# An earlier fetch of one scalar, and a weight decoding whose two engines run one step apart

## The chip, the cores and the metric

The kernel runs on one core of a Trainium2 chip. Its engines work side by side, each through its own list of instructions in order, and wait for each other by semaphores: TensorE (PE in the profile; PEld is its weight load) does the matrix products, VectorE (DVE) and ScalarE (ACT) the elementwise work, GpSimd (POOL) a little setup, and SyncE (SP) issues most transfers. The metric is the device time of one execution in microseconds (us). Three runs of the kernel before took 658.86, 659.36 and 659.38 us, so the median is 659.36.

## The reference

Attention with a soft cap over 2 batches, 12 heads, 448 positions and head size 64; its output, as 896 tokens of 768 features, goes through two gated layers of width 1536:

```
scores = cap * tanh((q @ k.T / sqrt(64)) / cap)
attn   = exp(scores - max);  attn = attn / (sum(attn) + 1e-9)
x      = attn @ v                                  # 896 x 768
x      = (silu(x @ g1) * (x @ v1)) @ o1            # layer 0
out    = (sigmoid(x @ g2) * (x @ v2)) @ o2         # layer 1
```

`cap` is one number. The six weight matrices arrive as 64-bit floats.

## The kernel before

**Precision.** Every operand of a large product is split in a high and a low part (names end in h and l), and three products are summed: high by high, low by high, high by low.

**Weights.** A block of a weight matrix (768 words of 64 bits in each of the 128 partitions, the tile `r`) is turned into its two 32-bit parts by `decode`, which VectorE and ScalarE share: VectorE shifts the top word (`t`, L74), ScalarE rounds it (`c`, L75), VectorE collects the remaining bits (`g`, L77 and L78) and puts the sign back (`c`, L80), ScalarE writes the high part (`wh`, L81), VectorE takes off the exponent and writes the low part (`wl`, L83 and L84). `decode` is a generator. Each of its `yield`s, and one more in `Stream.steps`, ends a step, so a block has four steps. `ws.step()` emits one step; `ws.through(key)` emits all steps up to the end of that block. When a block is done, the load of the block after the next one is issued on SyncE's queue. `("g", 0, 1)` is the gate block of layer 0, columns 128 to 255; `("v", 0, 1)` is the value block of the same columns.

**Attention.** The 24 heads are worked on in 12 pairs (`for i in range(NPAIR)`). For each pair TensorE transposes K and Q (`transposed`), VectorE and ScalarE split them (`qk_parts`: `kh`, `qh`, `kl`, `ql`), TensorE makes the scores of four key chunks (`scores`), ScalarE puts tanh on them with the scale `inv_sb`, which is made from the cap on VectorE (L467 to L471), and then the exponential in two parts (`exponentials`); VectorE adds up exponentials (`sums`), TensorE multiplies with V (`values`: `pv`, and the denominators `pd`), ScalarE and VectorE take the results out of PSUM (`taken_off`: `xu`, `dn`). The denominators travel through memory: `g` is fetched from `dn`, inverted, written to `d` and read back spread over the partitions as `rb` (`inverted`); `normalized` multiplies and splits the result into `xh` and `xl`. The loop is pipelined: in the turn of pair i the sums and values are those of pair i-1, the inversion that of i-2, the normalization that of i-3, the transposes those of i+2. The order of the calls in the loop is the order of the instructions on each engine.

From pair 3 on (`FIRST`), some steps of the weight decoding are emitted in each turn, `NS` = 16 in all: four blocks.

**The passage to the layers.** After the loop the first products of layer 0 are interleaved with the last pair: the gate block over the first batch's tokens, the last pair's values, the value block over the first batch, then both over the second batch (first without the last two pairs), the second gate block over the first batch, and only then the part that needs the last two pairs. `inverted_here(last)` inverts the last denominators on VectorE directly.

**The layers.** TensorE runs without a pause, and the other engines decode blocks ahead of it with `ws.through`.

Of the kernel before, what the change touches and what calls it, by code (L numbers as in the profile page):

```python
# [9 lines left out]
F32 = mybir.dt.float32  # L10
# [9 lines left out]
def attention_then_two_gated_layers(  # L20
# [14 lines left out]
    nc = tc.nc  # L35
# [3 lines left out]
    P = 128  # L39
# [9 lines left out]
    const = ctx.enter_context(tc.tile_pool(name="const", bufs=1))  # L49
# [16 lines left out]
    def decode(r, hi, lo):  # L66

        n = r.shape[1] * r.shape[2]
        w2 = r.rearrange("p k f -> p (k f)").bitcast(U32).rearrange("p (n two) -> p n two", two=2)
        low, top = w2[:, :, 0], w2[:, :, 1]  # L70
        t = wp.tile([P, n], U32, tag="t", name="t", bufs=1)
        c = wp.tile([P, n], U32, tag="c", name="c", bufs=2)
        g = wp.tile([P, n], F32, tag="g", name="g", bufs=1)
        nc.vector.tensor_scalar(t, top, 0x7FFFFFFF, 9, ALU.bitwise_and, ALU.logical_shift_right)  # L74
        nc.scalar.activation(c, t, AF.Relu, bias=bias_sb, scale=4096.0)  # L75
        yield
        nc.vector.tensor_scalar(g.bitcast(U32), top, 0x1FF, None, ALU.bitwise_and)  # L77
        nc.vector.scalar_tensor_tensor(g, low, 2.0**-32, g.bitcast(U32), ALU.mult, ALU.add)  # L78
        yield
        nc.vector.scalar_tensor_tensor(c, top, 0x80000000, c, ALU.bitwise_and, ALU.bitwise_or)  # L80
        nc.scalar.copy(hi, c.bitcast(F32).rearrange("p (k f) -> p k f", k=r.shape[1]))  # L81
        yield
        nc.vector.tensor_scalar(t, c, 0xFF800000, None, ALU.bitwise_and)  # L83
        nc.vector.scalar_tensor_tensor(  # L84
            lo,
            g.rearrange("p (k f) -> p k f", k=r.shape[1]),
            2.0**-20,
            t.bitcast(F32).rearrange("p (k f) -> p k f", k=r.shape[1]),
            ALU.mult,
            ALU.mult,  # L90
        )

    class Stream:
# [11 lines left out]
        def load(self, upto):  # L105
            while self.loaded < min(upto, len(self.keys)):
                key = self.keys[self.loaded]
                src = self.jobs[key][0]
                r = wp.tile([P, src.shape[0] // P, src.shape[1]], I64, tag="r", name="r", bufs=2)
                nc.sync.dma_start(r, src.rearrange("(k p) f -> p k f", p=P))  # L110
                self.raw[key] = r
                self.loaded += 1
# [37 lines left out]
    def products(o, w, bh, bl, u, ks, nk, off=0):  # L150

        for kk in ks:
            for m, (a, x) in enumerate(((w[0], bh), (w[0], bl), (w[1], bh))):
                nc.tensor.matmul(  # L154
                    o,
                    lhsT=a[:, kk - off, :],
                    rhs=x[:, kk, halves[u]],
                    start=(kk == 0 and m == 0),
                    stop=(kk == nk - 1 and m == 2),
                )  # L160
# [8 lines left out]
    def weights():  # L169
        pools, z_tiles = {}, {}  # L170

        def z_part(eb, c):
            def get():
                if eb not in z_tiles:
                    if eb == 0:
                        z_tiles[eb] = [pools["hp"].tile([P, KF, ZB[0]], F32R, name=n) for n in ("zh0", "zl0")]
                    else:
                        z_tiles[eb] = [const.tile([P, KF, ZB[1]], F32R, tag=n, name="z" + n) for n in ("xh", "xl")]
                return [z[:, :, c * ZW : (c + 1) * ZW] for z in z_tiles[eb]]

            return get

        jobs = {}

        def z_job(eb, c):
            e0 = sum(ZB[:eb]) + c * ZW
            jobs["z", eb, c] = (o2[:, e0 : e0 + ZW], z_part(eb, c))

        for layer, (wg, wv) in enumerate(((g1, v1), (g2, v2))):
            for f in range(KF):  # L190
                for kind, w in (("g", wg), ("v", wv)):
                    jobs[kind, layer, f] = (w[:, f * P : (f + 1) * P], None)
                if (layer, f) in early:
                    z_job(0, early.index((layer, f)))
            if layer == 0:
                for e in range(KD):
                    for part in range(2):
                        if part == 0 and (2, e) in early:
                            z_job(0, early.index((2, e)))
                        jobs["o", e, part] = (o1[part * KD * P : (part + 1) * KD * P, e * P : (e + 1) * P], None)  # L200
        for c in range(ZB[1] // ZW):
            z_job(1, c)
        return Stream(jobs), pools, z_tiles
# [93 lines left out]
    ws, pools, z_tiles = weights()  # L297
    with ExitStack() as actx:
        ap = actx.enter_context(tc.tile_pool(name="ap", bufs=2))
        dr = actx.enter_context(tc.tile_pool(name="dr", bufs=2, space=bass.MemoryType.DRAM))  # L300
        fix = actx.enter_context(tc.tile_pool(name="fix", bufs=1))

        warm = ap.tile([P, 512], mybir.dt.bfloat16, tag="x", name="warm", bufs=2)
        nc.vector.memset(warm, 0.0)
# [36 lines left out]
        def load_v(i):  # L341
            b, p = pairs[i]
            tv = vt[i % NV]
            nc.sync.dma_start(tv[:, :, :NB], v[b, 2 * p : 2 * p + 2, :S0].rearrange("h (p r) d -> p h r d", r=NB))
            for j in range(2):
                nc.sync.dma_start(tv[rows[j], j, NB, :], v[b, 2 * p + j, S0:])
# [48 lines left out]
        def sums(i, part):  # L395

            e = ex[i]
            if part == 0:
                es[i] = ap.tile([P, 2, S], F32, tag="es", name="es", bufs=2)
                nc.vector.tensor_tensor(es[i], e[:, 0:2], e[:, 2:4], ALU.add)  # L400
            else:
                nc.vector.tensor_tensor(es[i], es[i], e[:, 4:6], ALU.add)
# [32 lines left out]
        def inverted(i):  # L435
            g = dens.pop(i)
            nc.vector.reciprocal(g, g)
            d = dr.tile([2 * S], F32, tag="d", name="d")
            nc.sync.dma_start(d.rearrange("(p c) -> p c", p=CP), g)
            rb[i] = ap.tile([P, S], F32, tag="rb", name="rb", bufs=2)  # L440
            for j in range(2):
                nc.sync.dma_start(rb[i][rows[j]], d[j * S : (j + 1) * S].unsqueeze(0).to_broadcast([D, S]))

        def inverted_here(i):

            xu[i], d = nd.pop(i)
            rb[i] = ap.tile([P, S], F32, tag="rb", name="rb", bufs=2)
            nc.vector.reciprocal(rb[i], d)

        def normalized(i):  # L450
            b, p = pairs[i]
            x = ap.tile([P, S], F32, tag="x", name="x", bufs=2)
            nc.vector.tensor_tensor(x, xu.pop(i), rb.pop(i), ALU.mult)
            o = slice(b * S, (b + 1) * S)
            nc.vector.tensor_copy(xh[:, p, o], x)
            nc.vector.tensor_tensor(xl[:, p, o], x, xh[:, p, o].bitcast(F32), ALU.subtract)

        cap_sb = const.tile([P, 1], F32, name="cap_sb")
        nc.gpsimd.dma_start(cap_sb, cap.to_broadcast([P, 1]))
        wide_sb = const.tile([1, 1], mybir.dt.int32, name="wide_sb")  # L460
        inv_sb = fix.tile([P, 1], F32, name="inv_sb")
        near_sb = const.tile([P, 1], F32, name="near_sb")
# [9 lines left out]
        qk_parts(0)  # L472
        load(2)
        load_v(1)
        NS, FIRST = 16, 3
        for i in range(NPAIR):
            if i + 3 < NPAIR:
                load(i + 3)
            if i + 2 < NPAIR:
                load_v(i + 2)  # L480
            if i == 1:
                ws.load(2)
            if i > 0:
                sums(i - 1, 1)
            if i > 1:
                inverted(i - 2)
            if i > 2:
                normalized(i - 3)
            scores(i, 0)
            if i == 0:  # L490
                transposed(1)
                qk_parts(1, nc.vector.tensor_copy)
            scores(i, 1)
            exponentials(i, 0)
            if i > 0:
                values(i - 1)
            if i >= FIRST:
                n = NPAIR - FIRST
                for _ in range(NS * (i - FIRST) // n, NS * (i - FIRST + 1) // n):
                    ws.step()  # L500
            sums(i, 0)
            if i > 0:
                taken_off(i - 1)
            scores(i, 2)
            scores(i, NB)
            exponentials(i, 1)
            if i + 2 < NPAIR:
                transposed(i + 2)
                qk_parts(i + 2, nc.vector.tensor_copy)
# [7 lines left out]
        products(begun[0][0][0], w0[0], xh, xl, 0, range(KD), KD)  # L517
        values(last)
        products(begun[0][1][0], w0[1], xh, xl, 0, range(KD), KD)
        inverted_here(last)  # L520
        normalized(last)
        normalized(last - 1)
# [112 lines left out]
```

## Time and profile before

| | before |
|---|---|
| median of 3 runs | 659.36 us |
| the profiled execution's own time | 659.29 us |
| span of its profile (first to last instruction) | 657.5 us |
| PE busy | 642.7 us (98%) |
| DVE busy | 459.1 us (70%) |
| ACT busy | 276.0 us (42%) |
| mean granted TensorE clock | 0.99 of full |

Times of the trace count from the span's start. The rows below are of four kinds. A timeline row gives the start, the duration, the engine, the line, what is written from what, and in brackets the idle time of the engine just before and what ended it; "xN" is N instructions merged. A waits row gives total us, times and the longest. A windows row gives, for a stretch, its length, each engine's busy time, the granted clock (1.00 is 2.4 GHz, 0.50 is 1.2 GHz) and the DMA engines' share. A group row gives the count, the summed busy time and the mean of one in ns. Most of the span is the layers, where TensorE is busy throughout; the attention takes about the first 116 us.

### The profile page before, as it was taken

What the parts mean: (1) busy time and instruction counts of PE and PEld (TensorE: products, weight loads), DVE (VectorE), ACT (ScalarE), POOL (GpSimd) and SP (SyncE); (2) the same over time, 40 slices, a digit from 0 to 9 for tenths busy, and PEclk for the clock granted to TensorE, in tenths of its full rate; (3) what the DMA queues carried; (4) which work ended last, traced back from release to release, by engine and by line L of the source; (5) the groups of instructions that cost most, each with busy time, mean ns of one, the idle gap of its engine ahead of it and who ended that gap; (6) DMA issues with size and microseconds to landing.
All of it is one profiled execution on the core that took longest, in us unless ns stands there. A gap on an engine that the chain in (4) does not pass through costs nothing. (4 is left out here: it accounts for less than half of the span.)

```text
span 657.5 us, 8373 instructions
## 1 busy us (share of the span) xinstructions
PE 642.7 (98%) x3311; PEld 548.3 (83%) x3311; DVE 459.1 (70%) x678; ACT 276.0 (42%) x352; POOL 3.9 (1%) x25
## 2 busy tenths in 40 slices
PE   7999899999999999999999999999999999999996
PEld 4455454799999999999999999999999999999995
DVE  3689899648798777886969767777887773693000
ACT  2988699224344333443434324333443332342000
POOL 2000000000000000000000000000000000000000
PEclk7999899999999999999999999999999999999999
DMA  5644442204433234433344233334342332270111
GB/s 138 196 112 129 110 127 78 65 20 135 134 113 128 96 107 133 134 130 122 112 129 144 97 118 119 100 110 130 99 141 97 97 124 68 67 224 21 43 28 34
DMA packets 99861, 70.86 MB, mean 108 GB/s; under 512 B 29030, under 2 KB 99814, under 8 KB 99814
## 3 DMA queue, kind: packets, MB, share of 16 engines
q1 hardware_dynamic: 98662, 69.80, 34.8%
q8 instruction: 28, 0.46, 0.3%
q10 hardware_dynamic: 1120, 0.45, 0.3%
q14 instruction: 19, 0.16, 0.1%
q0 software_dynamic: 32, 0.00, 0.0%
HBM read 67.40 MB, written 2.79 MB: 107 GB/s over the span
## 5 line engine op out<-in xcount | busy, mean ns | idle before, releaser
L75 ACT ACTIVATE c<-t,bias_sb 128x768 uint32<-128x768 uint32 x72 | 67.7, 940 | 87.1 <-DVE t L74 87.1
L81 ACT CAST wh<-c 128x768 fp32r<-128x768 f32 x60 | 50.3, 839 | 81.2 <-DVE c L80 81.1
L78 DVE SCALAR_TENSOR_TENSOR g<-r,g 128x768 f32<-128x768 uint32 x72 | 69.0, 959 | 2.5
L80 DVE SCALAR_TENSOR_TENSOR c<-r,c 128x768 uint32<-128x768 uint32 x72 | 68.5, 951 | 0.8 <-ACT c L75 0.7
L227 DVE TENSOR_TENSOR sg<-pv,sg 128x448 f32<-128x448 f32 x48 | 29.8, 620 | 49.5 <-PE pv L154 41.6
L84 DVE SCALAR_TENSOR_TENSOR wl<-g,t 128x768 fp32r<-128x768 f32 x60 | 57.5, 959 | 2.1
L228 ACT CAST hh<-sg 128x448 fp32r<-128x448 f32 x48 | 27.2, 567 | 74.2 <-DVE sg L227 74.2
L154 PE MATMUL pg<-xh,wh 128*128 128x448 f32 x144 | 52.8, 367 | 0.3 <-ACT e L385 0.3
L154 PE MATMUL pg<-hl,wh 128*128 128x448 f32 x144 | 53.0, 368 | 0.0
L154 PE MATMUL pg<-hh,wl 128*128 128x448 f32 x144 | 53.0, 368 | 0.0
L154 PE MATMUL pg<-hh,wh 128*128 128x448 f32 x144 | 53.0, 368 | 0.0
L154 PE MATMUL pv<-xh,wh 128*128 128x448 f32 x144 | 52.8, 367 | 0.0
L154 PE MATMUL pv<-yh,wl 128*128 128x448 f32 x144 | 52.7, 366 | 0.0
L154 PE MATMUL pg<-xl,wh 128*128 128x448 f32 x144 | 52.7, 366 | 0.0
L154 PE MATMUL pg<-yh,wh 128*128 128x448 f32 x144 | 52.7, 366 | 0.0
L154 PE MATMUL pg<-yl,wh 128*128 128x448 f32 x144 | 52.7, 366 | 0.0
L154 PE MATMUL pv<-yl,wh 128*128 128x448 f32 x144 | 52.7, 366 | 0.0
L154 PE MATMUL pg<-xh,wl 128*128 128x448 f32 x144 | 52.7, 366 | 0.0
L154 PE MATMUL pg<-yh,wl 128*128 128x448 f32 x144 | 52.7, 366 | 0.0
L154 PE MATMUL pv<-xh,wl 128*128 128x448 f32 x144 | 52.7, 366 | 0.0
L154 PE MATMUL pv<-yh,wh 128*128 128x448 f32 x144 | 52.7, 366 | 0.0
L154 PE MATMUL pv<-xl,wh 128*128 128x448 f32 x144 | 52.7, 366 | 0.0
(98 smaller groups left out, 1274.1 us busy)
## 6 DMA issues: line engine op xcount, KB each, us to landing
r<-in_moe_w_gate_dram SPq DMA_DIRECT2D x24, 768.0 KB, 4.4
r<-in_moe_w_val_dram SPq DMA_DIRECT2D x24, 768.0 KB, 4.2
r<-in_moe_w_out_dram SPq DMA_DIRECT2D x24, 768.0 KB, 4.4
tq<-in_q_dram SPq DMA_DIRECT2D x11, 224.0 KB, 4.0
rb<-d SPq DMA_DIRECT2D x22, 112.0 KB, 2.9
kt<-in_k_dram SPq DMA_DIRECT2D x12, 192.0 KB, 3.2
vt<-in_v_dram SPq DMA_DIRECT2D x12, 192.0 KB, 3.4
out_dram<-ob SPq DMA_DIRECT2D x4, 140.0 KB, 3.7
```

The source lines that it names most:

```text
L75: nc.scalar.activation(c, t, AF.Relu, bias=bias_sb, scale=4096.0)
L78: nc.vector.scalar_tensor_tensor(g, low, 2.0**-32, g.bitcast(U32), ALU.mult, ALU.add)
L80: nc.vector.scalar_tensor_tensor(c, top, 0x80000000, c, ALU.bitwise_and, ALU.bitwise_or)
L81: nc.scalar.copy(hi, c.bitcast(F32).rearrange("p (k f) -> p k f", k=r.shape[1]))
L84: nc.vector.scalar_tensor_tensor(lo, g.rearrange("p (k f) -> p k f", k=r.shape[1]), 2.0**-20, t.bitcast(F32).rearrange("p (k f) -> p k f", ...
L154: nc.tensor.matmul(o, lhsT=a[:, kk - off, :], rhs=x[:, kk, halves[u]], start=(kk == 0 and m == 0), stop=(kk == nk - 1 and m == 2),)
L227: nc.vector.tensor_tensor(sg, vs[u], sg, ALU.mult)
L228: nc.scalar.copy(hh[:, f, halves[u]], sg)
```

## The change

Four edits. The transfer of the cap is the first thing that GpSimd does, ahead of its memory fills. In `decode` the first `yield` stands before ScalarE's rounding instead of behind it, and the third before ScalarE's copy, so that ScalarE's instruction comes in the step after VectorE's that it reads; a block still has four steps. `NS` is 8 instead of 16, so the loop decodes two blocks, and the second gate block is decoded after the loop, ahead of the last inversion, with the second value block behind the last normalizations as the existing call places it. In the loop `normalized(i - 3)` is called ahead of `inverted(i - 2)`.

```
         nc.vector.tensor_scalar(t, top, 0x7FFFFFFF, 9, ALU.bitwise_and, ALU.logical_shift_right)
+        yield
         nc.scalar.activation(c, t, AF.Relu, bias=bias_sb, scale=4096.0)
-        yield
         nc.vector.tensor_scalar(g.bitcast(U32), top, 0x1FF, None, ALU.bitwise_and)
...
         nc.vector.scalar_tensor_tensor(c, top, 0x80000000, c, ALU.bitwise_and, ALU.bitwise_or)
+        yield
         nc.scalar.copy(hi, c.bitcast(F32).rearrange("p (k f) -> p k f", k=r.shape[1]))
-        yield
...
+        cap_sb = const.tile([P, 1], F32, name="cap_sb")
+        nc.gpsimd.dma_start(cap_sb, cap.to_broadcast([P, 1]))
...
-        cap_sb = const.tile([P, 1], F32, name="cap_sb")
-        nc.gpsimd.dma_start(cap_sb, cap.to_broadcast([P, 1]))
...
-        NS, FIRST = 16, 3
+        NS, FIRST = 8, 3
...
+            if i > 2:
+                normalized(i - 3)
             if i > 1:
                 inverted(i - 2)
-            if i > 2:
-                normalized(i - 3)
...
         products(begun[0][1][0], w0[1], xh, xl, 0, range(KD), KD)
+        ws.through(("g", 0, 1))
         inverted_here(last)
```

Lines below L303 are one or two higher in the changed kernel. ScalarE in the turn of pair 6, before, from the first exponentials to the tanh of the next scores:

```order
L391 ACTIVATE e<-e,near_sb 128x1792
L81 CAST wh<-c 128x768
L429 COPY xu<-pv 128x448
L385 ACTIVATE e<-pss,inv_sb 128x896
L385 ACTIVATE e<-pss,inv_sb 128x448
L391 ACTIVATE e<-e,near_sb 128x1344
```

The same place in the changed kernel (pair 6), with the turn of pair 7 up to its copy of `pv`:

```order
L393 ACTIVATE e<-e,near_sb 128x1792
L431 COPY xu<-pv 128x448
L387 ACTIVATE e<-pss,inv_sb 128x896
L387 ACTIVATE e<-pss,inv_sb 128x448
L393 ACTIVATE e<-e,near_sb 128x1344
L387 ACTIVATE e<-pss,inv_sb 128x896 x2
L393 ACTIVATE e<-e,near_sb 128x1792
L82 CAST wh<-c 128x768
L431 COPY xu<-pv 128x448
```

The write of `wh` stands one turn behind the step of VectorE that makes its `c`. VectorE in the turn of pair 6, before:

```order
L402 TENSOR_TENSOR es<-es,e 128x896
L437 RECIPROCAL g<-g 112x8
L453 TENSOR_TENSOR x<-xu,rb 128x448
L455 CAST xh<-x 128x448
L456 TENSOR_TENSOR xl<-x,xh 128x448
L77 TENSOR_SCALAR g<-r 128x768
L78 SCALAR_TENSOR_TENSOR g<-r,g 128x768
L80 SCALAR_TENSOR_TENSOR c<-r,c 128x768
L400 TENSOR_TENSOR es<-e 128x896
```

VectorE in the turn of pair 6, changed:

```order
L404 TENSOR_TENSOR es<-es,e 128x896
L455 TENSOR_TENSOR x<-xu,rb 128x448
L457 CAST xh<-x 128x448
L458 TENSOR_TENSOR xl<-x,xh 128x448
L439 RECIPROCAL g<-g 112x8
L80 SCALAR_TENSOR_TENSOR c<-r,c 128x768
L402 TENSOR_TENSOR es<-e 128x896
```

One decoding instruction stands there in place of three, and the small reciprocal has moved behind the normalization. VectorE after the loop, before, from the last sum to the end of the normalization of the last pair:

```order
L402 TENSOR_TENSOR es<-es,e 128x896
L437 RECIPROCAL g<-g 112x8
L453 TENSOR_TENSOR x<-xu,rb 128x448
L455 CAST xh<-x 128x448
L456 TENSOR_TENSOR xl<-x,xh 128x448
L448 RECIPROCAL rb<-pd 128x448
L453 TENSOR_TENSOR x<-pv,rb 128x448
```

The same place, changed:

```order
L404 TENSOR_TENSOR es<-es,e 128x896
L439 RECIPROCAL g<-g 112x8
L455 TENSOR_TENSOR x<-xu,rb 128x448
L457 CAST xh<-x 128x448
L458 TENSOR_TENSOR xl<-x,xh 128x448
L74 TENSOR_SCALAR t<-r 128x768
L77 TENSOR_SCALAR g<-r 128x768
L78 SCALAR_TENSOR_TENSOR g<-r,g 128x768
L80 SCALAR_TENSOR_TENSOR c<-r,c 128x768
L83 TENSOR_SCALAR t<-c 128x768
L84 SCALAR_TENSOR_TENSOR wl<-g,t 128x768
L450 RECIPROCAL rb<-pd 128x448
```

A whole block is decoded ahead of the last large reciprocal; the six instructions of another one stand behind the last normalization.

## Rows read from the trace of the kernel before

**Rows 1.** Waits of PE over the whole span: us in total, times, longest.

```profile
PE pss L384 <- ACT e L385: 4.4, 5, 1.8
PE pss L384 <- DVE kh L366: 2.7, 1, 2.7
```

**Rows 2.** Timeline of the first 16 us: GpSimd, TensorE, VectorE and ScalarE.

```profile
4.64 0.67 POOL L459 DMA_DIRECT2D cap_sb<-in_cap_dram  x1
5.82 0.60 PE L356 MATMUL pk<-ident,kt 128*128 128x128 f32 x4
8.02 0.16 DVE L467 TENSOR_TENSOR inv_sb<-cap_sb 128x1 f32<-128x1 f32 x1 [6.83 <-DMA cap_sb<-in_cap_dram]
8.72 0.68 DVE L366 CAST kh<-pk 128x512 fp32r<-128x512 f32 x1
10.72 0.73 PE L384 MATMUL pss<-ql,kh 64*128 64x448 f32 x2
14.71 1.01 ACT L385 ACTIVATE e<-pss,inv_sb 128x896 f32<-128x896 f32 x1 [2.20 <-PE pss L384]
15.74 1.79 ACT L391 ACTIVATE e<-e,near_sb 128x1792 f32<-128x1792 f32 x1
```

**Rows 3.** Windows at the start: length, busy us by engine, clock, DMA share, GB/s.

```profile
10.00:16.00 6.00, 6.00 (x27) 4.14 (x26) 3.10 (x6) 2.27 (x3) 0.00 (x0) 0.50 0.67 162
16.00:18.00 2.00, 1.55 (x11) 1.24 (x11) 0.43 (x1) 2.00 (x2) 0.00 (x0) 1.00 0.70 187
```

**Rows 4.** Timeline of TensorE in a later turn, transposes and the scores behind them.

```profile
34.59 0.60 PE L356 MATMUL pk<-ident,kt 128*128 128x128 f32 x4
...
36.01 0.36 PE L384 MATMUL pss<-ql,kh 64*128 64x448 f32 x2
```

**Rows 5.** Windows over three stretches of the attention (PE, PEld, DVE, ACT, POOL).

```profile
40.00:48.50 8.50, 8.50 (x57) 4.56 (x55) 7.02 (x13) 7.89 (x9) 0.00 (x0) 1.00 0.44 103
67.00:80.00 13.00, 11.21 (x61) 5.32 (x59) 12.37 (x20) 9.27 (x10) 0.00 (x0) 0.87 0.38 98
88.00:96.50 8.50, 8.50 (x57) 4.55 (x55) 8.40 (x15) 7.88 (x9) 0.00 (x0) 1.00 0.21 57
```

**Rows 6.** Waits of ScalarE for VectorE from 25 to 125 us.

```profile
ACT wh L81 <- DVE c L80: 5.2, 3, 2.6
ACT c L75 <- DVE t L74: 2.3, 4, 1.3
```

**Rows 7.** Timeline of ScalarE: first exponentials of pairs 3 and 11, one weight copy.

```profile
38.80 1.79 ACT L391 ACTIVATE e<-e,near_sb 128x1792 f32<-128x1792 f32 x1
...
70.66 0.83 ACT L81 CAST wh<-c 128x768 fp32r<-128x768 f32 x1 [2.62 <-DVE c L80]
...
111.85 1.79 ACT L391 ACTIVATE e<-e,near_sb 128x1792 f32<-128x1792 f32 x1
```

**Rows 8.** Groups of decoding instructions from 25 to 125 us, by form.

```profile
L78 DVE SCALAR_TENSOR_TENSOR g<-r,g 128x768 f32<-128x768 uint32 x4 | 3.8, 959 | 0.1
L74 DVE TENSOR_SCALAR t<-r 128x768 uint32<-128x768 uint32 x4 | 2.2, 562 | 0.0
L75 ACT ACTIVATE c<-t,bias_sb 128x768 uint32<-128x768 uint32 x4 | 3.8, 938 | 2.3 <-DVE t L74 2.3
```

**Rows 9.** Timeline of VectorE and TensorE in the passage to the layers.

```profile
124.78 2.96 DVE L448 RECIPROCAL rb<-pd 128x448 f32<-128x448 f32 x1 [3.90 <-PE pd L416]
...
137.00 0.36 PE L154 MATMUL pg<-xh,wh 128*128 128x448 f32 x1
...
139.00 0.62 DVE L227 TENSOR_TENSOR sg<-pv,sg 128x448 f32<-128x448 f32 x1 [7.89 <-ACT sg L226]
```

**Rows 10.** Timeline of SyncE's queue and VectorE in the turns of pairs 3 and 4.

```profile
41.30 1.43 SPq L442 DMA_DIRECT2D rb<-d  x2
...
47.11 0.57 DVE L453 TENSOR_TENSOR x<-xu,rb 128x448 f32<-128x448 f32 x1
```

**Rows 11.** DMA issues of the page: count, KB each, median us to landing.

```profile
rb<-d SPq DMA_DIRECT2D x22, 112.0 KB, 2.9
```

## The prediction

> **What bounds the kernel now.** I read the waits of TensorE first, since it is busy 98% of the time: the whole span has only two kinds of wait of weight, 2.7 us once for VectorE's first `kh`, and 4.4 us in five pieces for ScalarE's tanh [rows 1]. All of them lie in the attention. So there are two things to win there and nothing behind it: in the layers TensorE never stops, and a change can only lose there.
>
> The first wait is at the start. VectorE stands idle for 6.83 us until the cap lands, at 8.02, because the small instructions on the cap come ahead of `kh` in its order; `kh` starts at 8.72 although its transposes were done at 5.82 + 0.60 = 6.42 [rows 2]. The cap's transfer was issued at 4.64, behind all of GpSimd's fills, and took 3.38 us. The idle TensorE then pays a second time: from 10 to 16 us it runs at a granted clock of 0.50, which is 1.2 GHz, and comes back to 2.4 GHz in the two microseconds after [rows 3].
>
> The second is in the loop. A turn in which TensorE is full takes 8.50 us, all of it busy (the first and the third of [rows 5]). The first exponentials start at 38.80 for pair 3 and at 111.85 for pair 11 [rows 7]: 73.05 us for eight turns, where eight full ones are 68.0. The 5.05 us between them are what the loop loses. Who takes them is seen at ScalarE: it stands 5.2 us before its copy to `wh` and 2.3 us before its rounding to `c`, each time for VectorE's instruction of the same turn [rows 6], the worst being 2.62 us at 70.66 [rows 7]. Behind it in ScalarE's order are the copy of `pv` and the next tanh, for which TensorE waits 1.8 us at most [rows 1]; after that wait the clock falls again (0.87 as a mean of 13 us, so 0.13 x 13 / 0.5 = 3.4 us at half speed) [rows 5].
>
> **The cap first.** The transfer takes 3.38 us and the small instructions on it 0.70 us (8.02 to 8.72). For `kh` to start when its transposes are done, at 6.42, the issue must come before 6.42 - 0.70 - 3.38 = 2.34. It is now GpSimd's first work behind the program's opening; I take 0.8 us (an estimate, since the fills that ran ahead of 4.64 run behind it), so there are 1.5 us to spare. `kh` then starts at about 6.46, which is 8.72 - 6.46 = 2.26 us earlier. GpSimd's fills come 0.67 us later, and the earliest of them is needed by the transposes at 5.82.
>
> What follows depends on the clock. If it falls as before, everything is 2.26 us earlier and nothing more. If it holds, the chain to the first exponentials shrinks: the product `ql,kh` starts 2.00 us after `kh` (10.72 - 8.72, set by VectorE), at 8.46; the next transposes a third of a microsecond later, at 8.8 (half of what 0.73 for the pair of products makes at the low clock); from the start of transposes to the end of the scores behind them a full-speed turn takes 36.01 + 0.36 - 34.59 = 1.78 us [rows 4], so 10.57; tanh and its successor need 15.74 - 14.71 = 1.03 us [rows 2], and the exponentials start at about 11.65 instead of 15.74: 4.09 us earlier. From there to the next turns ScalarE is the full engine (2.00 of 2.00 us busy from 16 to 18 [rows 3]), so the shift is kept. I take 4.09, because the idle of TensorE that goes before the slow stretch shrinks from 2.7 to about 0.5 us, and the row from 16 to 18 us shows TensorE busy only 1.55 of 2.00 us and yet at a clock of 1.00. The ends are 2.26 and 4.09.
>
> The Trainium skill speaks to this in "TensorE: Matmul & The Clock Gate", section "What's actually happening": the slow state is the default, activity releases it, and how many products run slow at the start varies from run to run. No single row here can show that variation; by it the slow stretch at the start may return in some executions, which is the low end above.
>
> **One step behind, and fewer steps.** A block costs VectorE three instructions of 0.96 us and three of 0.56 us [rows 8] (the ones not shown are of the same two kinds), 4.56 us, or 1.14 a step on average. Nine turns with 16 steps are 1.78 steps a turn, 2.03 us; with 8 steps, 0.89 and 1.01 us. The turn of pair 3, which has one step of 0.56 us, has VectorE 7.02 us busy of 8.50 [rows 5], so 6.46 without decoding. Before: 6.46 + 2.03 = 8.49 of 8.50, which leaves no room for any order but the luckiest. After: 7.5 on average, and at most 6.46 + 1.52 = 7.98 in a turn with `g` twice or `t` and `wl`. ScalarE keeps at most one decoding instruction in a turn, which is what it has in the full turn of pair 3 (7.89 of 8.50 busy, with 0.94 for `c` [rows 5, 8]). And that instruction now reads what VectorE made a turn ago, so the 7.5 us of [rows 6] go altogether. I take the whole 5.05 us. The bounds are 0, if VectorE holds TensorE up in another way, and 5.05, since a turn cannot be shorter than TensorE's 8.50.
>
> **Normalization ahead of the reciprocal.** No instruction is added. The reciprocal of pair i-2 comes later by three instructions of which the first takes 0.57 us [rows 10], at most 1.7 us (estimate), and with it the writing of `d` and the reading of `rb` on SyncE's queue, and the fetch of `g` and the loads of K and Q queued behind. `rb` is issued in two pieces from 41.30 and lands 2.9 us after its issue [rows 10, 11]: the second piece by about 42.3 + 2.9 = 45.2. It is used at 47.11, now at 47.0. So 1.8 us are to spare and at most 1.7 are used. I cost it at nothing; a few tenths of lateness would be taken up by VectorE's new slack.
>
> **The two blocks moved behind the loop.** TensorE has products there, and VectorE has gaps: 3.90 us before the large reciprocal at 124.78 and 7.89 us before 139.00 [rows 9], so its normalizations end at 131.11. In before's times the gate block takes 4.56 us of the first gap (ScalarE's `c` fits in: 0.56 + 0.94 is less than the 0.56 + 0.56 + 0.96 that VectorE does meanwhile), so the reciprocal and the normalizations come 0.66 us later and end at 131.8. TensorE needs them at 137.00 [rows 9], 5.2 us later. The value block then ends at 136.3, ahead of VectorE's next work at 139.00 and of its product, which comes later still. Its raw load follows the last step in the loop, not long after 111.85 [rows 7]. The price is nothing, and 5.2 us of cover would have to go before there is one.
>
> **Sum.** The profiled execution took 659.29 us, 1.8 of it outside its span of 657.5; that stands 0.07 under the median of 659.36. 659.29 - 4.09 - 5.05 = 650.15 us. I say 650.2.
>
> **Rivals.** *The clock falls at the start all the same:* 659.29 - 2.26 - 5.05 = 652.0. For it: TensorE still waits for `kh`, `kl` and `ql` in turn. Against: the row from 16 to 18 us above.
>
> *The loop gives half:* VectorE is late in some turns, by `rb` or by a step of 1.52 us that meets the exponentials late, and a long wait brings the slow clock again: 659.29 - 4.09 - 2.5 = 652.7. Against: the turn with 8.40 us of VectorE [rows 5] kept TensorE full.
>
> *The start gives nothing,* since the cap's transfer, issued among the first loads, lands no earlier: 659.29 - 5.05 = 654.2; with nothing in the loop either, the change doesn't do what it says and the time stays within 0.2% (1.3 us, about what a measurement here can tell from no change).
>
> *Slower:* the new order closes a ring: the normalization waits for `rb`, behind it on VectorE the reciprocal waits, behind that `d`, and then the next `rb`. Its round took 45.2 - 38.6 = 6.6 us (38.6 being 47.1 less a turn) and is now up to 8.3 of the 8.50. If transfers landed 1.6 us later than the median in every turn, a turn would be 8.3 + 1.6 = 9.9, eight of them 11.2 us more than full ones, and the time 659.29 - 9.14 + 11.2 = 661.4. It decides from 1.3 us of lateness a turn on. Against: the DMA engines were 44% and 21% busy in the full turns [rows 5].
>
> **How the numbers follow.** My forecast 56%, by itself 649.4 to 651.0; the low clock 19%; half the loop 12%; nothing at the start 5%; no change 4%; slower 4%. Faster is the sum of the first four, 92%. The range must hold the first two and most of the third: 649.2 to 653.4, with some 17% outside.
>
> **What would show it.** In the profile after: `kh` at about 6.5 with no wait for the cap; a clock of 1.00 from 10 to 16; first exponentials at about 11.7; from pair 3 to pair 11, 68.0 us between the first exponentials; no wait of ScalarE for `c` or `t` in the loop; no wait of TensorE before 137 - 9 = 128 or behind it. I am wrong if the clock row at the start is 0.50 again, if VectorE waits for `rb` in the loop, or if TensorE waits for `xh` in the passage.

## The result, and the profile after

The changed kernel takes 650.97 us (median of five runs, 650.72 to 654.87), against 659.26 us for the kernel before beside it (five runs, 656.71 to 659.38). The ratio is 0.9906, with a 95% interval from 0.9883 to 0.9929, so it is faster by 4.7 to 7.7 us of the 659.26. The two medians, 8.29 us apart, would by themselves give 0.9874, below that interval: three of the five changed runs lie at 650.7 to 651.0, the other two at 653.1 and 654.9. The profiled execution took 650.72 us of its own, 1.8 of it outside its span of 648.9. Against the 659.29 of the profile before that is 8.57 us less.

Three instants divide this difference: the first exponentials of pairs 0, 3 and 11, and the first product of the layers.

| | before | after | difference | forecast |
|---|---|---|---|---|
| first exponentials, pair 0 | 15.74 | 12.34 | -3.40 | -4.09 |
| pair 3 to pair 11 (eight turns) | 73.05 | 69.49 | -3.56 | -5.05 |
| first product of the layers | 116.14 | 109.19 | -6.95 in all | -9.14 in all |
| from there to the last product's start | 534.88 | 533.17 | -1.71 | 0 |

So in these two profiles the change gave 6.95 us where it acts, 2.2 less than forecast, and 1.71 us came from a place that no edit touches; together they are 0.09 more than the 8.57, which lies behind the last product's start and in rounding. The first three rows are the change's; the last is taken up in the section on the hardware. The 6.95 us lie inside the interval of the ratio; the 9.14 of the forecast, a ratio of 0.9861, do not.

The start, on VectorE and ScalarE of the changed kernel, with GpSimd's transfer and TensorE's first transposes (timeline, start and duration in us; compare [rows 2]):

```profile
1.24 0.67 POOL L303 DMA_DIRECT2D cap_sb<-in_cap_dram  x1 [0.78 <-POOLq L618]
...
4.49 0.16 DVE L467 TENSOR_TENSOR inv_sb<-cap_sb 128x1 f32<-128x1 f32 x1 [3.31 <-DMA cap_sb<-in_cap_dram]
...
6.34 0.63 PE L358 MATMUL pk<-ident,kt 128*128 128x128 f32 x4 [0.23 <-POOLq L539]
...
7.00 0.69 DVE L368 CAST kh<-pk 128x512 fp32r<-128x512 f32 x1 [1.73 <-PE pk L358]
...
12.34 1.79 ACT L393 ACTIVATE e<-e,near_sb 128x1792 f32<-128x1792 f32 x1
```

The cap is there at 4.49, long before `kh` needs it, and what ends VectorE's idle time ahead of `kh` is now the transposes. These come at 6.34, half a microsecond later than before. The windows of the changed kernel (length, busy us of PE, PEld, DVE, ACT and POOL, clock, DMA share, GB/s) answer to [rows 3] and, with the loop as one window, to [rows 5]:

```profile
3.00:4.00 1.00, 1.00 (x4) 0.36 (x3) 0.00 (x0) 0.40 (x1) 0.73 (x5) 1.00 0.25 54
...
10.00:16.00 6.00, 4.49 (x38) 3.55 (x38) 4.19 (x7) 5.16 (x6) 0.00 (x0) 1.00 0.66 161
...
35.39:104.88 69.49, 68.19 (x422) 35.51 (x420) 57.52 (x95) 58.00 (x59) 0.00 (x0) 1.00 0.39 103
```

From 10 to 16 us the granted clock is 1.00 (2.4 GHz), where it was 0.50. In the eight turns VectorE is busy 57.52 of 69.49 us, and the clock is 1.00 throughout. The same stretch of the kernel before:

```profile
38.80:111.85 73.05, 69.60 (x422) 36.16 (x420) 65.07 (x107) 61.64 (x63) 0.00 (x0) 0.98 0.43 116
```

TensorE waits for ScalarE's `e` 1.8 us in all now, in place of 4.4 [rows 1], and nearly all of it lies in the first turns. In the loop the waits of the changed kernel are these (total us, times, longest; TensorE from 25 to 125 us and VectorE from 21 to 125):

```profile
PE pd L418 <- DVE es L404: 1.0, 2, 0.6
PE pss L386 <- ACT e L387: 0.3, 1, 0.3
```

```profile
DVE x L455 <- DMA rb<-d: 7.9, 7, 2.0
...
DVE g L439 <- DMA g<-dn: 3.3, 2, 1.9
```

ScalarE's waits for VectorE's decoding [rows 6] are gone from the loop. In their place VectorE itself waits for the denominators' transfers, 7.9 us for `rb`. Two turns come out long: 60.89 to 70.00 and 95.53 to 104.88, 9.11 and 9.35 us in place of 8.50. In each of them TensorE stands for VectorE's `es` (0.38 us at 62.62, 0.62 at 97.49). How the wait for `rb` gets there can be followed for the first:

```profile
54.52 0.63 DVE L455 TENSOR_TENSOR x<-xu,rb 128x448 f32<-128x448 f32 x1 [1.96 <-DMA rb<-d]
...
56.81 0.96 DVE L78 SCALAR_TENSOR_TENSOR g<-r,g 128x768 f32<-128x768 uint32 x1
...
61.48 1.08 DVE L404 TENSOR_TENSOR es<-es,e 128x896 f32<-128x896 f32 x1
...
62.62 0.97 PE L418 MATMUL pd<-es,ones 128*64 128x448 f32 x4 [0.38 <-DVE es L404]
```

VectorE has stood 1.96 us for `rb`, has the longest step of the decoding in that turn (L77 and L78), works without a pause up to `es`, and is late with it. The second long turn has the same before it: 1.34 us for `rb` up to 89.39, then L77 and L78. The wait of 1.84 us up to 45.51 has no such step behind it and holds TensorE up nowhere.

### The profile page after: what moved, and what is told of

Same layout as the page of the kernel before. It is cut to its first block, busy times and chain, and to the rows that moved or that the text cites. A ratio compares the mean times of both kernels' runs of the same rounds, so it can differ in the third digit from the quotient of the medians.

```text
span 648.9 us, 8385 instructions
## 1 busy us (share of the span) xinstructions
PE 637.4 (98%) x3311; PEld 545.7 (84%) x3311; DVE 459.3 (71%) x678; ACT 276.0 (43%) x352; POOL 4.0 (1%) x25
## 5 line engine op out<-in xcount | busy, mean ns | idle before, releaser
L78 DVE SCALAR_TENSOR_TENSOR g<-r,g 128x768 f32<-128x768 uint32 x72 | 69.0, 959 | 2.5
L84 DVE SCALAR_TENSOR_TENSOR wl<-g,t 128x768 fp32r<-128x768 f32 x60 | 57.5, 958 | 2.1
```

The lines of the kernel that those rows point to most:

```text
L84: nc.vector.scalar_tensor_tensor(lo, g.rearrange("p (k f) -> p k f", k=r.shape[1]), 2.0**-20, t.bitcast(F32).rearrange("p (k f) -> p k f", ...
```

## The experiments

Each was timed beside the kernel before on the same chip. "Start" is the start of the first exponentials of pair 0 (15.74 before, 12.34 changed), "first product" that of the first product of the layers (116.14 before, 109.19 changed), and the loop is pair 3 to pair 11, as above; all three are of one profiled execution of each kernel.

| kernel | median us | ratio, 95% interval | start | loop | first product |
|---|---|---|---|---|---|
| changed kernel again | 652.03 | 0.9874 to 0.9910 | 12.37 | 69.81 | 109.55 |
| cap only | 657.72 | 0.9971 to 0.9998 | 12.60 | 74.30 | 114.24 |
| order put back | 653.07 | 0.9898 to 0.9930 | 12.35 | 69.98 | 109.67 |
| decoding only | 654.45 | 0.9918 to 0.9948 | 15.98 | 68.00 | 111.30 |
| shift only | 660.23 | 1.0009 to 1.0035 | 15.98 | 74.34 | 117.67 |
| fewer steps only | 656.11 | 0.9957 to 0.9987 | 15.90 | 69.53 | 112.77 |
| TensorE filled | 658.03 | 0.9969 to 0.9995 | 13.85 | 72.52 | 113.72 |
| ring on GpSimd's queue | 652.07 | 0.9890 to 0.9921 | 12.04 | 68.01 | 107.42 |
| cap behind three fills | 652.94 | 0.9884 to 0.9919 | 12.07 | 71.79 | 111.22 |
| raw loads on GpSimd's queue | 654.81 | 0.9910 to 0.9953 | 12.44 | 68.00 | 111.10 |
| both of these | 655.65 | 0.9924 to 0.9965 | 12.17 | 68.22 | 111.63 |
| one raw load later | 652.31 | 0.9894 to 0.9937 | 12.12 | 69.39 | 108.83 |

**The changed kernel again** (no edit), to see what repeats.

> The changed kernel again, beside the others on one chip, for their comparison. Theory (waits for rb in the loop, whose length differs from run to run): a median of 650.7 to 651.5 and a spread of some us again. Rival (the long runs were an accident): all runs within 1 us.

Start and loop repeat within 0.4 us, and the waits for `rb` come back (6.7 us in 6 times). TensorE stands for `es` three times here (0.17, 0.29 and 0.65 us), and only the last time has the turn before it the step of L77 and L78 behind its wait for `rb`; an earlier wait of 1.60 us with that step behind it holds TensorE up nowhere. So the step adds to the lateness, but it is the sum of a turn's delays that counts. The part behind the first product does not repeat: 534.89 in place of 533.17. The medians of this set are 6.90 us apart (658.93 and 652.03), those of the first set 8.29.

**The cap alone.** The kernel before with one edit:

```
+        cap_sb = const.tile([P, 1], F32, name="cap_sb")
+        nc.gpsimd.dma_start(cap_sb, cap.to_broadcast([P, 1]))
         warm = ap.tile([P, 512], ...)
```

> Before, with the cap's transfer issued first and nothing else changed. Theory (the late cap costs a wait of about 2 us and a further 1.4 to 1.6 us of slow clock behind it): first exponentials near 12.3 us as in the changed kernel, clock 1.00 from 10 to 16 us, time 659.3 - 3.4 = 655.9. Rival (the clock falls at the start whatever the cap does, and the decoding edits raised it): only the wait goes, first exponentials near 14.0, time 657.6. Both: the slow turns of pairs 4 to 7 are still there, 73 us from pair 3 to pair 11.

The start comes 3.14 us earlier (15.74 to 12.60) and the clock is 1.00 from 10 to 16 us, but the loop grows from 73.05 to 74.30, the first product gains only 1.90, and the median 1.21 (658.93 to 657.72), where 3.4 was expected. ScalarE still waits for VectorE's `c` (6.5 us, 3 times, in place of 5.2), and TensorE for ScalarE's `e` (6.2 us over the whole span, in place of 4.4). I read it so that an earlier start is worth its full size only if what feeds the loop comes earlier too; this run alone does not show it.

**The decoding alone:** the kernel before with the shifted steps, eight of them, and the gate block behind the loop, but the cap late and the old order.

```
-        NS, FIRST = 16, 3
+        NS, FIRST = 8, 3
...
+        ws.through(("g", 0, 1))
         inverted_here(last)
```

> Before, with the decoding edits alone: ScalarE's part one step behind, two blocks in the loop, the second gate block ahead of the last reciprocal; the cap's transfer and the order of reciprocal and normalization as before. Theory (the loop's loss goes entirely with these): 68.0 us from pair 3 to pair 11, time 659.3 - 5.0 = 654.3, clock 0.50 from 10 to 16 us as before. Rival (VectorE holds TensorE up in another way): 70.5 us, time 656.8.

The loop is 68.00 us, eight turns of exactly 8.50: the 5.05 us of the forecast to the hundredth. In the loop VectorE waits nowhere for `rb`, and ScalarE not for VectorE:

```profile
39.01:107.01 68.00, 67.70 (x422) 35.75 (x420) 57.55 (x96) 57.97 (x59) 0.00 (x0) 1.00 0.38 101
```

The six runs lie within 0.62 us (654.16 to 654.78).

**The two halves of it.** Shift only: the `yield`s moved, `NS` still 16.

```
         nc.vector.tensor_scalar(t, top, ...)
+        yield
         nc.scalar.activation(c, t, AF.Relu, bias=bias_sb, scale=4096.0)
-        yield
```

> Before, with ScalarE's part of the decoding one step behind and nothing else: still 16 steps, four blocks, in the loop. Theory (the loop's 5 us are ScalarE's waits for VectorE's instruction of the same turn): those waits go from 7.5 us to under 2, the first exponentials of pair 11 come 68 to 69.5 us behind those of pair 3 instead of 73, time 654.3 to 655.8. Rival (VectorE's work, 8.49 of 8.50 us a turn, is what costs, whatever the order): 72 to 73 us, time 658 to 659.

Fewer steps only: `NS` 8 and the gate block behind the loop, the `yield`s where they were.

> Before, with two blocks decoded in the loop instead of four, the second gate block decoded ahead of the last reciprocal, and the decoding steps cut as before. Theory (the order costs): ScalarE still waits for VectorE's instruction of the same turn, in half as many turns, half of the loss remains, 70.5 us from pair 3 to pair 11, time 656.8. Rival (VectorE's work costs): 68.0 us, time 654.3, as with the order changed too.

The loop as one window, shift only, then fewer steps only:

```profile
39.02:113.36 74.34, 69.60 (x422) 36.38 (x420) 64.71 (x107) 61.35 (x63) 0.00 (x0) 0.98 0.41 113
```

```profile
38.95:108.48 69.53, 67.78 (x422) 35.74 (x420) 57.51 (x96) 59.07 (x60) 0.00 (x0) 1.00 0.37 97
```

With the shift alone the turns are clean up to 73.02 (before, the first long one began at 47.30) and then take 10.56, 11.62 and 9.63 us. VectorE falls behind there: TensorE stands 1.85 us for its `es` at 76.20, VectorE itself 2.75 us for `g` at 86.84, and behind that ScalarE 3.77 us for `t` at 89.14, although `t` now belongs to the step before. The loop is no shorter than before, and by the interval of its ratio the kernel is a little slower. With eight steps and no shift, one turn is long (81.45 to 91.92), and the rest are clean. So the load on VectorE (64.7 or 57.5 us in the eight turns) counts most. On top of the lower load the shift is worth 1.53 us of the loop (69.53 to 68.00); the ratios to before, 0.9972 and 0.9933 on two chips, agree in sign. That the wait for an instruction of the same turn was the whole loss fell.

**The order put back:** the changed kernel with the small reciprocal ahead of the normalization again.

```
+            if i > 1:
+                inverted(i - 2)
             if i > 2:
                 normalized(i - 3)
-            if i > 1:
-                inverted(i - 2)
```

> The changed kernel with the reciprocal put back ahead of the normalization. Theory (the normalization now waits for rb, seven waits of 7.9 us in all, and these delay the sums that TensorE waits for): no wait of VectorE for rb in the loop, 68.0 us from the first exponentials of pair 3 to those of pair 11 instead of 69.5, time 650.7 - 1.5 = 649.2, and less spread between runs than 650.7 to 654.9. Rival (the two long turns have another cause, VectorE's decoding or the loads of raw weights): 69.5 us again, time 650.7, same spread.

The wait for `rb` goes and one for `g` takes its place: 7.9 us in 6 times, up to 3.5, and TensorE then stands 1.7 us for `es` in one turn of 10.45. The median is 653.07 against 652.03 for the changed kernel on the same chip, but the runs of the two overlap (652.33 to 654.12, 650.56 to 653.05), and the two profiled executions, which have the same part behind the first product, are 0.14 us apart (653.01 and 652.87). So the swap may be worth up to 1 us, as it may be worth nothing, and it is not the cause of what the loop lost.

This kernel is also the decoding-only one with the early cap as its single difference, beside it on the same chip. The cap brings the start 3.63 us earlier (15.98 to 12.35) and lengthens the loop from 68.00 to 69.98; at the first product 1.63 us are left, and in the medians 1.38 (654.45 to 653.07), without overlap. Put on the kernel before, it kept 1.90 and 1.21. So of the 3.1 to 3.6 us that the cap gives at the start, the loop takes 1.2 to 2.0 back, with either decoding, while the decoding edits are worth 4.84 us at the first product with the late cap and 4.57 with the early one (4.48 and 4.65 in the medians).

**TensorE filled:** the kernel before with eleven more products on the warm-up tile behind the first transposes (their results are not used), the cap still late.

```
         transposed(0)
+        for _ in range(11):
+            nc.tensor.matmul(pw, lhsT=warm[:, :P], rhs=warm, start=True, stop=True)
```

> Before, with 11 more products of the warm-up kind (results unused) behind the first transposes, so that TensorE is busy for some 2.3 of the 2.7 us in which it waits for kh; the cap is as late as before. Theory (the slow clock from 10 to 16 us comes from that idle time): clock 1.00 from 10 to 16, first exponentials 1.4 to 1.8 us earlier, at 13.9 to 14.4, time 657.6 if the loop keeps the gain. Rival (the slow stretch is there anyway, for example because the products behind it are sparse): clock 0.50, 15.7, 659.3.

The window from 10 to 16 us:

```profile
10.00:16.00 6.00, 5.02 (x35) 3.65 (x35) 3.15 (x6) 4.17 (x4) 0.00 (x0) 1.00 0.70 167
```

`kh` starts at 8.54, nearly as late as before (8.72), and yet the clock holds at 1.00 and the exponentials come 1.89 us earlier. So the low clock of [rows 3] belonged to TensorE's idling before `kh`, and not to the thin work behind it. The other profiles agree: from 10 to 16 us the clock is 0.50 to 0.53 in the four with the late cap and nothing to fill the wait, and 0.99 or 1.00 in the nine with the early cap. The profiled execution is the fastest of the twelve (655.23); two more lie beside it (655.27 and 655.48), most near 658, and what those do is not seen.

**The ring on GpSimd's queue:** the changed kernel with the write of `d` and the two reads of `rb` issued by GpSimd instead of SyncE.

```
-            nc.sync.dma_start(d.rearrange("(p c) -> p c", p=CP), g)
+            nc.gpsimd.dma_start(d.rearrange("(p c) -> p c", p=CP), g)
...
-                nc.sync.dma_start(rb[i][rows[j]], ...)
+                nc.gpsimd.dma_start(rb[i][rows[j]], ...)
```

> The changed kernel, with the writing of d and the reading of rb issued on GpSimd's queue instead of SyncE's (three transfers a turn). Theory (with the start 3.4 us earlier, SyncE's queue is what the loop waits for: it issues without a pause up to 22 us, its turns of 8.8 to 9.2 us are longer than TensorE's 8.50, and the wait for d stands in it): SyncE's turns fall under 8.5, VectorE's waits for rb and g go, 68.0 us from pair 3 to pair 11, time 649.2, small spread. Rival (the transfers themselves are late, not their issue): VectorE waits for rb or g as before, 69.5 to 70, time 650.7 to 652.

The loop is 68.01 us and the first product comes 8.72 us earlier than before, close to the 9.14 of the forecast. The queue's own waits, changed kernel and then this one (SPq is SyncE's queue, 25 to 100 us):

```profile
SPq L444 <- DMA d<-g: 11.1, 8, 1.7
SPq L441 <- DVE g L439: 6.0, 2, 4.3
```

```profile
SPq L434 <- DVE dn L432: 26.9, 8, 6.7
SPq L434 <- DVE kh L368: 7.9, 1, 7.9
```

In the changed kernel SyncE stands 11.1 us for `d` to land, with the loads of K, Q and V and the next fetch of `g` queued behind it; here it stands 34.8 us in nine times ahead of its fetch of `g` for VectorE, that is, it is early. VectorE's waits for `rb` are 4.4 us in the loop, in place of 7.9 (a further 3.1 lies behind it), and none reaches TensorE. The median, 652.07, is not below the changed kernel's 652.03 on another chip, and 649.2 was expected. The profiled execution (650.08) has the short level of the layers (see the last section), and with the long one it would be 651.8; the other four lie from there up (651.84 to 652.61), which fits the long level but was not traced. So the profile shows the clean loop, and the runs do not tell this version from the changed kernel.

**The cap behind three fills** (its two lines moved behind `make_identity(nc, ident)` in the changed kernel):

> The changed kernel with the cap's transfer issued behind GpSimd's first three fills (those of the first transposes) instead of ahead of them, near 1.7 us instead of 1.24. Theory (in all kernels with the cap first, the DMA engines move 54 to 57 GB/s from 3 to 4 us where the others move 183 to 197, and the first transposes start at 6.3 instead of 5.8: the small transfer in front holds the first loads up): 180 GB/s or more from 3 to 4 us, transposes at 5.8, first exponentials at 11.8, and 0.5 us less time, 650.2 to 651.5 in the median. Rival (the loads are held up wherever the cap's transfer stands among them, or by something else): below 100 GB/s from 3 to 5 us, transposes at 6.3 or later, no gain.

```profile
3.00:4.00 1.00, 1.00 (x4) 0.37 (x3) 0.00 (x0) 0.37 (x1) 0.77 (x6) 1.00 0.76 172
```

From 3 to 4 us the DMA engines move 172 GB/s, in place of 54; `kh` starts at 6.74 and the first exponentials at 12.07, both 0.27 us earlier than changed. But two kernels with the cap first, the ring on GpSimd's queue and the one raw load later, start as early (`kh` at 6.72 and 6.78) with 74 GB/s there, so the place of the cap is not shown to be the reason. The loop of this profile takes 71.79 us, 2.30 more than in the changed kernel, and nothing is left of the 0.27; the median, 652.94, is above the 650.2 to 651.5 that were expected.

**The raw loads on GpSimd's queue**, for the first four blocks, in the changed kernel; then this together with the cap behind three fills.

```
-                nc.sync.dma_start(r, src.rearrange("(k p) f -> p k f", p=P))
+                queue = nc.gpsimd if self.loaded < 4 else nc.sync
+                queue.dma_start(r, src.rearrange("(k p) f -> p k f", p=P))
```

> The changed kernel with the four raw weight loads of the attention (768 KB each) issued on GpSimd's queue instead of SyncE's. Theory (what is late in the loop are small transfers queued behind these loads: g of the first pair is issued right behind 1.5 MB at 22.3 us, and the long turns follow the load at 77.5 us): the long turns go, 68.0 us from pair 3 to pair 11, median 650.2, spread under 1 us. Rival (SyncE's issuing or the transfers' round trip is late without them): waits for rb and g stay, 69 to 70 us, median 652 and a spread of 2 us.

> The changed kernel with both: the cap's transfer behind the first three fills and the four raw loads on GpSimd's queue. If both theories hold: transposes at 5.8, 68.0 us from pair 3 to pair 11, 659.3 - 4.1 - 5.05 = 650.1 or a little less, in nearly all runs. If neither does: 652 with the spread of the changed kernel.

In both the raw loads no longer wait for SyncE and run beside the first loads of K. TensorE's waits and the window of the first of the two:

```profile
PE pk L359 <- DMA kt<-in_k_dram: 3.3, 2, 2.7
```

```profile
10.00:16.00 6.00, 2.85 (x21) 1.88 (x19) 3.44 (x5) 5.16 (x6) 0.00 (x0) 0.99 0.96 289
```

The DMA engines are full from 10 to 16 us, the second pair comes at 21.33 instead of 18.82, the start's gain is gone, and the loop is then clean (68.00 and 68.22). A clean loop goes with a late third pair once more (38.80, as before the change); but SyncE has fewer issues here too, and which of the two makes it clean these two kernels do not show.

**One raw load later:** only one block's raw load ahead of the loop's first turns in the changed kernel, the other in turn 4.

```
             if i == 1:
-                ws.load(2)
+                ws.load(1)
...
+            if i == 4:
+                ws.load(2)
```

> The changed kernel with only the first raw weight load (768 KB) in the turn of pair 1 and the second one, whose block is decoded from pair 8 on, in the turn of pair 4, behind that turn's inversion. Theory (SyncE's queue issues without a pause up to 22 us in every kernel; in the changed one the 1.5 MB issued at 20.9 then holds up the transfers right behind them, and d of the first pair is issued at 30.7, only 0.5 us earlier than in the kernel without the early cap, 31.2, though the computing is 3.6 us ahead): d is issued before 29, VectorE's waits for rb are under 4 us instead of 6.7 to 7.9, 68.0 to 68.7 us from pair 3 to pair 11, median 650.2 to 650.9. Rival (a turn of SyncE's queue, 8.8 to 9.2 us, is too long whatever it starts with): the waits come back within a few turns, 69.5 us, median 652.

SyncE's first and seventh write of `d`, changed kernel (with one turn between) and then this one:

```profile
30.74 0.53 SPq L441 DMA_DIRECT2D d<-g  x1
...
51.04 1.12 SPq L444 DMA_DIRECT2D rb<-d  x2
...
57.48 0.52 SPq L441 DMA_DIRECT2D d<-g  x1
59.73 1.09 SPq L444 DMA_DIRECT2D rb<-d  x2
...
84.25 0.52 SPq L441 DMA_DIRECT2D d<-g  x1
```

```profile
27.37 0.53 SPq L441 DMA_DIRECT2D d<-g  x1
...
83.91 0.52 SPq L441 DMA_DIRECT2D d<-g  x1
```

The first `d` comes 3.4 us earlier, as I wanted, and by the seventh that is gone. In the decoding-only kernel, whose engines run 3.6 us behind, the seventh comes at 84.08. SyncE's own turn here is (83.91 - 27.37) / 6 = 9.4 us, against 8.9 in the changed kernel and 8.8 there (31.23 to 84.08), while TensorE's is 8.50. The longest of the six here, 46.07 to 56.67, has the load in it that was moved to turn 4. One turn of the queue is some 6.4 us of issuing, from the reads of `rb` (51.04) to the next write of `d` (57.48), and then the time until that `d` has landed and the next reads go out, 2.25 us here (59.73) and 1.8 to 3.1 in the other turns of the changed kernel. With a queue turn above 8.50 us the head start is used up. Of what was expected, `d` before 29 came true; VectorE's waits for `rb` (4.8 us), the loop (69.39) and the median (652.31) did not.

## Why the prediction was right, and where it was not

**Direction and size.** The forecast was 650.2 and the measured median 650.97, inside the forecast's own range of 649.2 to 653.4. That nearness is partly luck: where the change acts, it gave 6.95 of the 9.14 us, and 1.71 us of the layers made up for most of the rest. The second set of runs, at 652.03, stands nearer to what the change by itself gives. Of the signs that the forecast set for itself, the clock of 1.00 came, and ScalarE's waits left the loop; the 68.0 us did not come, and one of the three signs of being wrong did: VectorE waits for `rb` in the loop.

**The start, 4.09 forecast, 3.40 measured.** The mechanism held: the cap no longer holds `kh`, and the clock stayed at 1.00, so it was the far end of the two that I gave. The filled TensorE shows that the idle time is the cause of the low clock. The 0.69 us that are missing have two parts. `kh` came at 7.00 and not 6.46, because the transposes started at 6.34 and not 5.82. I had asked only whether GpSimd's fills would be in time for them, not whether the transfers of K would. What delays them is not settled: over the kernels with the early cap `kh` starts between 6.72 and 7.29, wherever the cap stands among the fills. The chain from `kh` to the exponentials took 5.34 us, where I had 5.19; my own terms add up to 5.14, since 10.57 and 1.03 make 11.60 and not 11.65.

**The loop, 5.05 forecast, 3.56 measured.** The decoding edits by themselves are worth the whole 5.05 us (68.00 in the decoding-only kernel). My reason was half right. I read the loss off ScalarE's waits [rows 6] and argued that the shift removes them. Alone it puts them off and gains nothing; the other argument of the same paragraph, that VectorE had 8.49 of 8.50 us to do, carried most of it (69.53 with the fewer steps alone).

**What failed: two steps that were each priced alone.** "From there to the next turns ScalarE is the full engine, so the shift is kept" and "1.8 us are to spare and at most 1.7 are used" cannot both stand. It is the first that fails: in both pairs of kernels that differ by the cap alone, the 3.1 and 3.6 us at the start are 1.9 and 1.6 at the first product. The second was reckoned at the times of before: `rb` there by 45.2, used at 47.0. With the start 3.4 us earlier, VectorE asks for it 3.4 us earlier. The row of the changed kernel:

```profile
45.51 0.63 DVE L455 TENSOR_TENSOR x<-xu,rb 128x448 f32<-128x448 f32 x1 [1.84 <-DMA rb<-d]
```

`rb` came at 45.51, near the 45.2 worked out, and VectorE was ready at 45.51 - 1.84 = 43.67. SyncE's queue did not follow the engines: it issues without a gap up to 22 us in the changed kernel, so the earlier start does nothing for what stands at its end, and afterwards its turn is the longer one. That is the rival "the loop gives half" in its mechanism, with 12%; it named `rb` and a decoding step of 1.52 us as alternatives, and in both long turns of this profile the one came on top of the other. It is not the rival in its price: it assumed 2.5 us lost and a slow clock, and the loop lost 1.49 us at a clock of 1.00. The ring on GpSimd's queue points to the cause from the other side: with the ring's transfers off SyncE, the early start and the clean loop are there together, in the one execution that was traced; its median does not show a gain. SyncE's nine microseconds are made of both its issues (6.4 us) and the landing of `d`; what shortening either alone would give was not tried.

**The swap of normalization and reciprocal.** I forecast nothing, and the runs do not clearly show anything else: 0.12 us at the first product, 1.04 between medians whose runs overlap. With the reciprocal ahead, VectorE waits for `g`, one transfer earlier in the same ring. The slower rival, that the new order closes a ring and every turn grows to 9.9 us, fell: the longest of VectorE's waits for `rb` was 2.0 us, above the 1.3 from which it was to decide, but not in every turn.

**The tail at nothing** held. VectorE of the changed kernel behind the loop, answering to [rows 9]:

```profile
119.78 2.95 DVE L450 RECIPROCAL rb<-pd 128x448 f32<-128x448 f32 x1
...
125.47 0.63 DVE L458 TENSOR_TENSOR xl<-x,xh 128x448 fp32r<-128x448 f32 x1
...
129.53 0.96 DVE L84 SCALAR_TENSOR_TENSOR wl<-g,t 128x768 fp32r<-128x768 f32 x1
...
132.06 0.62 DVE L227 TENSOR_TENSOR sg<-pv,sg 128x448 f32<-128x448 f32 x1 [1.57 <-ACT sg L226]
```

The gate block is decoded from 115.38 to 119.86, the normalizations end at 126.10 and the value block at 130.49; VectorE still has 1.57 us of idle time ahead of `sg`, and TensorE waits for nothing between 110 and 640 us.

## What to carry to other kernels

When an edit brings the engines forward, go over each in-order queue that feeds them and ask when it can have its next item there: a queue that has been issuing without a gap does not come forward with them. Margins read from the old trace ("1.8 us to spare") shrink by that shift. And where an engine is loaded to 99% of a turn, take load away before moving waits about.

## What was not expected of the hardware

**One stretch of products runs at one of two rates.** Behind the first product the kernels take either 533.17 or 534.89 us, in all fourteen profiles, and nothing between. The difference lies in the output products of layer 0, from about 290 to 380 us. Windows of TensorE there, of the changed kernel and of the same kernel in its second set of runs:

```profile
290.00:375.00 85.00, 85.00 (x421) 78.77 (x420) 69.19 (x98) 31.62 (x41) 0.00 (x0) 1.00 0.39 123
```

```profile
290.00:375.00 85.00, 85.00 (x413) 77.23 (x412) 67.59 (x96) 30.77 (x40) 0.00 (x0) 1.00 0.38 123
```

Both are busy all of the 85 us at a clock of 1.00, without a wait, and yet one makes 421 products and the other 413: 0.202 against 0.206 us each. It is the same program, so the change has no part in it. What decides is open. It means that single times of one kernel can differ by 1.7 us for a reason that has nothing to do with an edit.

**The first loads move less beside an early cap.** In the microsecond from 3 to 4, while the first K and Q are on their way, the DMA engines move 53 to 74 GB/s in the seven profiles in which the cap is issued at 1.24 to 1.28 us, 172 and 179 in the two in which it is issued three fills later, and 183 to 213 in the five with the cap late. By what means 512 bytes hold the others up is open, and, as the starts above show, it is not the whole of what sets the first transposes.
